# Attention scores of the next step issued ahead of the second unit's own outputs, and the output copy split in two

## The chip, the cores and the metric

The kernel runs on one core of one Trainium2 chip. The metric is the device time of one execution in microseconds, as the median of three runs.

## The reference, cut to what matters

Two blocks follow each other. The first is a chunked state-space attention over 4 batches, 8 heads, 768 positions, head size 32 and state size 16; the kernel uses chunks of 128 positions, which gives the same result as the reference's chunks of 32:

```python
L = np.exp(cum[:, :, :, None] - cum[:, :, None, :]) * causal
M = np.einsum('bhin,bhjn->bhij', Cc, Bc) * L            # scores, masked and decayed
y_intra = np.einsum('bhij,bhjd->bhid', M, xc)           # a chunk's own outputs
y_inter = np.einsum('bhin,bhnd->bhid', Cc, state) * np.exp(cum)[..., None]
y[:, :, sl] = y_intra + y_inter
state = decay_full * state + sum_j(B_j x_j decay_from_j)
```

The second is a mixture of 8 experts: each of the 3072 tokens (256 wide) goes to the one expert with the largest gate logit, and gets `relu(x @ w1[e]) @ w2[e]` times its gate probability.

## The kernel before, in words

A *unit* is one chunk of 128 positions of one batch, with all 8 heads: 24 units. A *step* `d` handles the two units `2d` and `2d+1`; there are 12 steps (`ND`), and the first `NP = 2` of them have no earlier state. The order of every instruction on every engine is the order in which the Python code issues it (`manual_schedule`); semaphores are placed by the tile framework, which follows which instruction reads or writes what part of which tile.

One step on TensorE, in the order of the code before the change:

- `rows(d-1)` (line 347 of the profile, tile `r`): the outputs of the step before, turned back to token rows and multiplied with the gate weights. It reads the tile `yT`: first the half of heads 0 to 3 (`t = 0`) for both units, then the half of heads 4 to 7 (`t = 1`).
- `y_old(d)` (line 327): the part of the outputs from the carried state, into the PSUM tile `y`; from step 2 on.
- `rank` (lines 392 to 399), in six of the steps: places of the tokens within their expert.
- `y_own(d, 0)` (line 335): the first unit's own outputs, 8 matmuls, one for each head, from `M` and the scaled inputs `xp`. Each head takes 32 of the 128 output partitions, so that four heads lie beside each other.
- `own(d)` (line 292): the new state's sum, into a free part of `y` (`A_ps`). In steps 0 and 1 it stands ahead of the own outputs, in step 11 it is left out.
- `y_own(d, 1)` (line 335): the second unit's own outputs.
- `scores(2d+2)` and `scores(2d+3)` (line 277, tile `g`): the scores of the two units of the next step, 8 matmuls on quarters of 32 rows.

The other engines around it:

- VectorE: `weigh(2d)` and `weigh(2d+1)` (line 282) take the scores from `g`, mask them and write `M`; then `rows_out(d-1)` (line 357), logits, choices and ranks.
- ScalarE: masked `C` for the next step (line 261, tile `cm`), `faded` (line 303), in steps 7 to 9 the scaled inputs of the second unit of the next step (line 269), then `turned(d)` (line 340), which copies the outputs of both units from `y` to `yT` in one instruction, and `state(d)` (line 312), four small ones that write `S`. In step 4 `turn_both(1)` transposes two tables into `y` on TensorE before that copy, and `take_both(1)` (line 225) and the copy into `ew` (line 252) follow it on ScalarE.
- GpSimd: the other scaled inputs (line 271), the state's sum (line 318), and the indirect DMAs (line 421) that put token rows into per-expert lists in HBM.
- SP: all plain loads.

`g` and `y` exist once each. `g` is laid out as four banks, each with one half for even and one half for odd units; `y` as two banks, one for each half of four heads:

```python
g_ps = ps.tile([128, 4, 2, 256], FP32, name="g")       # bank q, unit parity, 2 heads x 128
y_ps = ps.tile([128, 2, 512], FP32, name="y")          # bank t, units side by side; A_ps and tables behind
A_ps = y_ps[:, 0, 256:384]
```

After step 11 come six filler matmuls (line 135) and the experts: for each, 8 blocks of `h` (line 551) and the products with `w2` (line 586), TensorE alone setting the pace.

Of the kernel before, what the change touches and what calls it, by code (L numbers as in the profile page):

```python
# [9 lines left out]
FP32 = mybir.dt.float32  # L10
# [8 lines left out]
NB, NH, S, D, NS = 4, 8, 768, 32, 16  # L19
N, DM, E, F = 3072, 256, 8, 1024  # L20
CH = 128
NP = NB // 2
NC = S // CH
ND = NP * NC
# [7 lines left out]
KT, FT = DM // 128, F // 128  # L32
# [15 lines left out]
def ssd_then_moe(ctx, tc, xs_in, ae_in, wgx, w_gate, w1, w2, gx, gb, gc, ga, out):  # L48
    nc = tc.nc
# [14 lines left out]
    wk = att.enter_context(tc.tile_pool(name="wk", bufs=2))  # L64
# [49 lines left out]
    y_ps = ps.tile([128, 2, 512], FP32, name="y")  # L114
# [17 lines left out]
    def idle(n, to=r_ps[:, 0]):  # L132

        for _ in range(n):
            nc.tensor.matmul(to[:, 0:256], lhsT=none_bf[:, 0:128], rhs=none_bf, start=True, stop=True)
# [44 lines left out]
    sd = [dict() for _ in range(ND)]  # L180
    carry = {}

    def load(n):
        t = ld.tile([128, XW], FP32, name="xs_n")
        if n > 3:
            nc.sync.dma_start(out=t, in_=xs_in[n])
        else:
            nc.sync.dma_start(out=t[:, 384:640], in_=xs_in[n][:, 384:640])
        s_ = st[n]
        s_["t"] = t  # L190
        s_["x"] = t[:, 0:256]
        s_["B"] = t[:, 256:384]
        s_["BT"] = t[:, 384:512]
        s_["CT"] = t[:, 512:640]
# [7 lines left out]
    def load_w(e, u, q):  # L202
        n = KT * F // 4
        nc.sync.dma_start(out=w_sb[e][u][:, q * n:q * n + n], in_=(w1, w2)[u][e, :, q * n:q * n + n])
# [14 lines left out]
    def turn_both(w):  # L219
        for j, rows_ in enumerate((cum[:, w], inv)):  # L220
            nc.tensor.transpose(y_ps[:, 1, 256 + CW * j:256 + CW * j + CW], rows_, ident[0:CW, 0:CW])
# [32 lines left out]
    def masked_C(n, dve=False):  # L254
        t = wk.tile([128, 2, CH], FP32, name="cm", bufs=4)
        for u in range(2):
            if dve:
                nc.vector.tensor_scalar(out=t[:, u], in0=st[n]["CT"], scalar1=par[:, u:u + 1], scalar2=None,
                                        op0=ALU.mult)
            else:  # L260
                nc.scalar.mul(t[:, u], st[n]["CT"], par[:, u:u + 1])  # L261
        st[n]["cm"] = t

    def scaled_x(n, eng):
        t = wk.tile([128, NH, D], FP32, name="xp", bufs=4)
        st[n]["xp"] = t.rearrange("p h d -> p (h d)")
        if eng is nc.scalar:
            for h in range(NH):
                nc.scalar.mul(t[:, h], st[n]["x"][:, D * h:D * h + D], Ei[:, n, h:h + 1])
            return  # L270
        eng.tensor_tensor(out=t, in0=st[n]["x"].rearrange("p (h d) -> p h d", d=D),  # L271
                          in1=bc(Ei[:, n, :, None], [128, NH, D]), op=ALU.mult)

    def scores(n):
        for q in range(4):
            r = slice(32 * q, 32 * q + 32)
            nc.tensor.matmul(g_ps[:, q, n % 2], lhsT=st[n]["BT"][r],  # L277
                             rhs=st[n]["cm"][r].rearrange("p u i -> p (u i)"), start=True, stop=True)
# [18 lines left out]
    def faded(d):  # L297

        if d // NP == NC - 1 or d < NP:
            return  # L300
        fa = wk.tile([128, 2, 2 * D], FP32, name="fa")
        for s in range(2):
            nc.scalar.mul(fa[:, s], carry[d][:, s], ew[:, 2 * d + s:2 * d + s + 1])
        sd[d]["fa"] = fa
# [11 lines left out]
    def whole(d):  # L316
        if "fa" in sd[d]:
            nc.gpsimd.tensor_tensor(out=carry[d + NP], in0=carry[d + NP], in1=sd[d]["fa"], op=ALU.add)
# [11 lines left out]
    def y_own(d, s, heads):  # L330
        n = 2 * d + s
        first = d // NP == 0 and s == 0
        for h in heads:
            o = D * (h % 4)
            nc.tensor.matmul(y_ps[o:o + D, h // 4, CH * s:CH * s + CH], lhsT=st[n]["xp"][:, D * h:D * h + D],  # L335
                             rhs=st[n]["M"][:, h], start=first, stop=True, skip_group_check=True)

    def turned(d):
        sd[d]["yT"] = wk.tile([128, KT, 2 * CH], FP32, name="yT")
        nc.scalar.copy(out=sd[d]["yT"], in_=y_ps[:, :, 0:2 * CH])  # L340

    rt = [(sm if i < CUT else sm2).tile([128, n, W], FP32, name=f"rows{i}") for i, n in enumerate(RGS)]
    grp = [g for g, n in enumerate(RGS) for _ in range(n)]
# [1 line left out]
    def rows(d, to=None):  # L345
        for t, s in [(t, s) for t in range(KT) for s in range(2)]:
            nc.tensor.matmul((to[s] if to else r_ps[:, s])[:, 256 * t:256 * t + 160], lhsT=sd[d]["yT"][:, t, CH * s:CH * s + CH],  # L347
                                 rhs=turn[:, t].rearrange("p e h -> p (e h)"), start=True, stop=True,
                                 skip_group_check=True)
# [65 lines left out]
    def counted(g, cs):  # L415
        nc.gpsimd.tensor_tensor(out=cnt[:, g + 1, :], in0=cnt[:, g, :], in1=cs, op=ALU.add)
# [13 lines left out]
    def place(k, apart=True):  # L430
        to_places(rt[grp[k]][:, k - R0[grp[k]], :], pos[:, k:k + 1], apart)
# [282 lines left out]
    with tc.manual_schedule():  # L714
# [37 lines left out]
        for d in range(ND):  # L752
            k = d - 1
            for n in (2 * d + 6, 2 * d + 7):
                if n < NU:
                    load(n)
            for j, at in enumerate(wq):
                if at == d:
                    load_w(j // 8, j % 8 // 4, j % 4)
            def some_place(apart=False):  # L760
                if todo:
                    place(todo.pop(0), apart)

            if d == 9:
                counted(*counting.pop(0))
            some_place(d == 8)
            if d == 8:
                counted(*counting.pop(0))
            if k >= 0:
                whole(k)  # L770
            if d != 7:
                some_place()
            if d + 1 < ND:
                for s in range(2):
                    masked_C(2 * d + 2 + s)
                scaled_x(2 * d + 2, nc.gpsimd)
                if d in (6, 8):
                    some_place()
                if not 7 <= d <= 9:
                    scaled_x(2 * d + 3, nc.gpsimd)  # L780
            faded(d)
            if 7 <= d <= 9:
                scaled_x(2 * d + 3, nc.scalar)
            if k >= 0:
                rows(k)
            if d < NP:
                own(d)
            if d == 0 or d == 4:
                totals(d // 4)
            if d == 0:  # L790
                idle(3)
            y_old(d)
            q = late.get(d)
            if q is not None:
                rank(q)
                if q == CUT - 1:
                    counts(CUT)
            weigh(2 * d)
            weigh(2 * d + 1)
            if d == 0:  # L800
                take_totals(0)
                inverse(0, p0, 4, 12)
            y_own(d, 0, range(NH))
            if d >= NP:
                own(d)
            y_own(d, 1, range(NH))
            if d == 4:
                turn_both(1)
            turned(d)
            if d == 4:  # L810
                take_both(1)
            state(d)
            if d + 1 < ND:
                for s in range(2):
                    scores(2 * d + 2 + s)
            if q is not None:
                ranked(q)
                if q == CUT - 1:
                    cut()
                todo += list(range(R0[q], R0[q] + RGS[q]))  # L820
                if d == 7:
                    some_place()
            if d == ND - 1:
                m_xT(0)
            if k >= 0:
                rows_out(k)
                if d == 4:
                    take_totals(1)
            if d == 0:
                route_consts()  # L830
            if k >= 0:
                logits_of(k)
            if d in ends:
                q = ends[d]
                choose(q)
                counting.append((q, count(q)))
                if d < 7:
                    counted(*counting.pop(0))
                late[d + 1] = q
            if d == 1:  # L840
                empty_consts()
                empty_last()
                decays(1)
                lasts(1)
            if d == 3:
                inverse_rows(1)
            if d == 9:
                while todo:
                    some_place(len(todo) == 1)
            if d == 10:  # L850
                m_load(0, (nc.sync, nc.scalar))
                m_load(1)
                for k in range(8):
                    load_w(2, *divmod(k, 4))
                weakest()
# [137 lines left out]
```

## Time and profile before

| | us |
|---|---|
| median of 3 runs | 247.48 |
| lowest, highest | 246.64, 249.29 |
| the profiled execution, its own time | 247.47 |
| its span, first to last instruction | 245.8 |
| attention, steps 0 to 11, until the first expert's matmul | 0 to 60.56 of the span |

| engine | busy us | share of the span |
|---|---|---|
| TensorE, matmuls | 237.3 | 97% |
| TensorE, weight loads | 201.3 | 82% |
| ScalarE | 92.7 | 38% |
| VectorE | 88.5 | 36% |
| GpSimd | 82.8 | 34% |

Shares are averages over two very different parts: ScalarE, VectorE and GpSimd do most of their work in the first 60 us. In the timeline each line has the start, the duration (from the first to the last of the merged instructions), the engine, the line of the kernel, the operation, the tiles written and read, the size, the count, and in brackets how long the engine was idle before and what ended that. `PE` is a matmul and `PEld` the weight load that belongs to it. A float32 matmul shows as two matmuls and two weight loads, so 8 of them count as x16.

### The profile page before, as it was taken

The numbers are of one execution on the slowest core, as the hardware profiler recorded it, in microseconds if no ns is written. First come the engines' busy times: TensorE is split into PE (matmuls) and PEld (weight loads), VectorE is DVE, ScalarE is ACT, GpSimd is POOL, SyncE is SP. The second block draws the span as 40 slices with busy tenths as digits, with TensorE's granted clock in tenths as the row PEclk, the third lists the DMA queues.
The fourth block names the chain that finished last, engine by engine and source line by source line (L and its number), as shares of the span: only waits on it lengthen the run. The fifth ranks groups of instructions, "written<-read, shape, count | busy, mean of one in ns | idle before, by whom it ended". The sixth has DMA issues, their size and how long they took to land. (4 is left out here: it accounts for less than half of the span.)

```text
span 245.8 us, 5525 instructions
## 1 busy us (share of the span) xinstructions
PE 237.3 (97%) x2021; PEld 201.3 (82%) x2021; DVE 88.5 (36%) x279; ACT 92.7 (38%) x312; POOL 82.8 (34%) x144
## 2 busy tenths in 40 slices
PE   8889899999999999999999999999999999999992
PEld 5567778777888888888888888888999969989781
DVE  4699879998520222020201102052316007040000
ACT  4656768981322224141422324131432502614200
POOL 2484688880038506060413330111113012013031
PEclk9999999999999999999999999999999999999999
DMA  6999979965932278696867779454303100001001
GB/s 174 327 328 323 332 250 302 291 263 102 274 141 97 112 144 274 189 256 217 235 243 213 272 168 311 87 99 82 73 13 68 32 15 29 27 4 40 3 16 45
DMA packets 36407, 39.75 MB, mean 162 GB/s; under 512 B 21947, under 2 KB 23806, under 8 KB 36352
## 3 DMA queue, kind: packets, MB, share of 16 engines
q1 hardware_dynamic: 32816, 30.24, 43.2%
q0 software_dynamic: 2880, 8.66, 9.3%
q8 instruction: 27, 0.44, 0.7%
q10 hardware_dynamic: 656, 0.18, 0.3%
q14 instruction: 28, 0.23, 0.3%
HBM read 29.72 MB, written 9.86 MB: 161 GB/s over the span
## 5 line engine op out<-in xcount | busy, mean ns | idle before, releaser
L551 PE MATMUL h_ps<-xT,w 128*128 128x256 f32 (+3 forms) x512 | 90.0, 334 | 0.3 <-ACT hT L628 0.3
L551 PEld LDWEIGHTS h_ps<-xT,w 128*128 128x128 f32 x512 | 80.8, 190 | 7.6 <-ACT hT L628 0.7
L586 PE MATMUL y_ps<-w,hT 128*128 128x256 f32 x384 | 85.1, 380 | 0.0
L586 PEld LDWEIGHTS y_ps<-w,hT 128*128 128x128 f32 x384 | 72.6, 190 | 10.5 <-issue 0.8
L564 POOL DMA_INDIRECT out_dram<-yo,lt x24 | 23.8, 991 | 58.1 <-DVE yo L571 31.3
L509 DVE TENSOR_REDUCE t_se<-t_sub 128x1 f32<-128x8 f32 (+1 forms) x20 | 3.3, 165 | 102.8 <-ACT t_sub L507 102.8
L560 ACT ACTIVATE hT<-h_ps 128x256 f32<-128x256 f32 x64 | 24.4, 384 | 29.4 <-PE h_ps L551 28.9
L282 DVE TENSOR_TENSOR M<-g,mask 128x1024 f32<-128x1024 f32 x24 | 28.2, 1218 | 3.8 <-PE g L277 3.6
L628 ACT ACTIVATE hT<-h_ps 128x128 f32<-128x128 f32 (+2 forms) x64 | 18.0, 292 | 24.1 <-PE h_ps L551 24.1
L421 POOL DMA_INDIRECT x_hbm<-rows,pos x24 | 23.9, 994 | 9.3 <-DVE pos L408 5.3
L573 ACT ACTIVATE yo<-y_ps,t_gt 128x256 f32<-128x256 f32 x14 | 6.6, 474 | 43.2 <-PE y_ps L586 43.2
L421 POOL DMA_INDIRECT x_hbm<-zrows,rest x8 | 7.7, 962 | 35.4 <-DMA lt<-x_hbm 24.9
L335 PE MATMUL y<-M,xp 128*32 128x128 f32 x384 | 15.3, 277 | 1.6 <-DVE M L282 1.3
L347 PEld LDWEIGHTS r<-turn,yT 128*128 128x128 f32 x88 | 12.2, 189 | 4.4 <-ACT yT L340 3.0
L261 ACT ACTIVATE cm<-xs_n,par 128x128 f32<-128x128 f32 x46 | 15.1, 419 | 1.5 <-DMA xs_n<-in_xs_dram 1.5
L347 PE MATMUL r<-turn,yT 128*128 128x160 f32 x88 | 14.9, 312 | 0.7 <-ACT ew L252 0.7
L564 POOL DMA_INDIRECT out_dram<-yh,lh x4 | 3.9, 983 | 33.1 <-ACT yh L602 21.2
L277 PE MATMUL g<-cm,xs_n 32*128 32x256 f32 x192 | 15.0, 423 | 0.0
L271 POOL TENSOR_TENSOR xp<-xs_n,Ei 128x256 f32<-128x256 f32 x20 | 12.1, 617 | 6.8 <-DVE last L241 3.6
L571 DVE TENSOR_SCALAR yo<-y_ps,t_gt 128x256 f32<-128x256 f32 x10 | 4.7, 483 | 24.2 <-PE y_ps L586 24.2
L340 ACT COPY yT<-y 128x512 f32<-128x512 f32 x12 | 7.0, 586 | 16.1 <-PE y L335 14.2
L520 DVE STREAM_TRANSPOSE xT<-xb 128x512 f32<-128x512 f32 (+1 forms) x16 | 9.8, 632 | 8.6 <-DMA xb<-x_hbm 7.1
(123 smaller groups left out, 156.2 us busy)
## 6 DMA issues: line engine op xcount, KB each, us to landing
w<-in_w_dram SPq DMA_DIRECT2D x64, 256.0 KB, 5.8
xs_n<-in_xs_dram SPq DMA_DIRECT2D x20, 320.0 KB, 5.8
xb<-x_hbm SPq DMA_DIRECT2D x30, 64.0 KB, 2.3
xb<-x_hbm SPq DMA_DIRECT2D x32, 48.0 KB, 2.4
xs_n<-in_xs_dram SPq DMA_DIRECT2D x4, 192.0 KB, 3.6
x_hbm<-zrows SPq DMA_DIRECT2D x1, 672.0 KB
lt<-x_hbm SPq DMA_DIRECT2D x8, 80.0 KB, 2.7
xs_n<-in_xs_dram SPq DMA_DIRECT2D x4, 128.0 KB, 2.3
```

Of the source, the lines that this page charges most:

```text
L261: nc.scalar.mul(t[:, u], st[n]["CT"], par[:, u:u + 1])
L271: eng.tensor_tensor(out=t, in0=st[n]["x"].rearrange("p (h d) -> p h d", d=D), in1=bc(Ei[:, n, :, None], [128, NH, D]), op=ALU.mult)
L277: nc.tensor.matmul(g_ps[:, q, n % 2], lhsT=st[n]["BT"][r], rhs=st[n]["cm"][r].rearrange("p u i -> p (u i)"), start=True, stop=True)
L282: nc.vector.tensor_tensor(out=t, in0=g_ps[:, :, n % 2].rearrange("p q (u i) -> p q u i", u=2), in1=bc(mask[:, None, None, :], [128, 4, 2, ...
L335: nc.tensor.matmul(y_ps[o:o + D, h // 4, CH * s:CH * s + CH], lhsT=st[n]["xp"][:, D * h:D * h + D], rhs=st[n]["M"][:, h], start=first, sto ...
L347: nc.tensor.matmul((to[s] if to else r_ps[:, s])[:, 256 * t:256 * t + 160], lhsT=sd[d]["yT"][:, t, CH * s:CH * s + CH], rhs=turn[:, t].rea ...
L421: s_ = nc.gpsimd.indirect_dma_start(out=x_hbm[:, :], out_offset=bass.IndirectOffsetOnAxis(ap=at, axis=0), in_=row, in_offset=None)
L551: nc.tensor.matmul(p[:, 0:n], lhsT=w[:, c:c + 128], rhs=xT[:, t, 0:n], start=(t == 0), stop=(t == KT - 1))
L560: nc.scalar.activation(ex[i]["hT"][:, f, 0:n], q, func=ACT.Relu)
L564: return nc.gpsimd.indirect_dma_start(out=out[:, :], out_offset=bass.IndirectOffsetOnAxis(ap=tok, axis=0), in_=yo[:, :], in_offset=None, b ...
L586: nc.tensor.matmul(p, lhsT=ex[i]["hT"][:, f, 128 * t:128 * t + 128], rhs=w_sb[e][1][:, f * DM:f * DM + DM], start=(f == 0), stop=(f == FT ...
L628: nc.scalar.activation(ex[i + u]["hT"][:, f, 0:n], q, func=ACT.Relu)
```

## The change

On TensorE the scores of the next step now stand between `own(d)` and `y_own(d, 1)`. The second unit's own outputs are issued in two halves of four heads, and each half is followed by its own copy into `yT`: 24 copies of 256 elements in place of 12 of 512. In step 4 the two table transposes come after the second half and ahead of its copy.

```diff
-    def turned(d):
-        sd[d]["yT"] = wk.tile([128, KT, 2 * CH], FP32, name="yT")
-        nc.scalar.copy(out=sd[d]["yT"], in_=y_ps[:, :, 0:2 * CH])
+    def turned(d, t):
+
+        if t == 0:
+            sd[d]["yT"] = wk.tile([128, KT, 2 * CH], FP32, name="yT")
+        nc.scalar.copy(out=sd[d]["yT"][:, t], in_=y_ps[:, t, 0:2 * CH])
...
             y_own(d, 0, range(NH))
             if d >= NP:
                 own(d)
-            y_own(d, 1, range(NH))
-            if d == 4:
-                turn_both(1)
-            turned(d)
+            if d + 1 < ND:
+                for s in range(2):
+                    scores(2 * d + 2 + s)
+            for t in range(KT):
+                y_own(d, 1, range(4 * t, 4 * t + 4))
+                if t == 1 and d == 4:
+                    turn_both(1)
+                turned(d, t)
             if d == 4:
                 take_both(1)
             state(d)
-            if d + 1 < ND:
-                for s in range(2):
-                    scores(2 * d + 2 + s)
```

## The prediction

> **What bounds the kernel now.** I read the windows first (which stage has slack on which engine), then the waits, then the timeline of single steps. The chain that ended last holds only the final store and says nothing here.
>
> ```profile
> core 0: us, PE busy (x) PEld busy (x) DVE busy (x) ACT busy (x) POOL busy (x), PEclk, DMA share, GB/s
> ...
> 30.00:40.00 10.00, 9.85 (x190) 7.98 (x190) 8.34 (x16) 6.74 (x28) 8.45 (x13) 1.00 0.84 266
> 40.00:50.00 10.00, 10.00 (x209) 7.76 (x207) 9.45 (x22) 9.87 (x42) 8.60 (x14) 1.00 0.94 314
> ```
> ```profile
> DVE M L282 <- PE g L277: 3.6, 7, 1.0
> ...
> PEld y L335 <- DVE M L282: 2.5, 5, 0.8
> ```
>
> The attention part (to 60.56 us) is a ring of nearly equal engines: from 30 us on TensorE has almost no gap, VectorE is over 80% busy, ScalarE full between 40 and 50. The two waits are all that TensorE and VectorE lose to each other over scores and `M`: VectorE 3.6 us, TensorE 2.5 us. From 60 us on TensorE is busy without a break (its listed idle there is some 2 us in 185), so a delay of attention comes out at the end one to one. A step of the ring (step 5, then step 6 up to its second unit):
>
> ```profile
> 33.00 0.40 PEld L335 LDWEIGHTS y<-M,xp 128*32 128x32 f32 x16
> ...
> 33.60 0.74 PEld L277 LDWEIGHTS g<-cm,xs_n 32*128 32x128 f32 x16 [0.20 <-issue]
> 33.60 1.15 PE L277 MATMUL g<-cm,xs_n 32*128 32x256 f32 x16
> ...
> 33.81 0.59 ACT L340 COPY yT<-y 128x512 f32<-128x512 f32 x1 [2.08 <-PE y L335]
> ...
> 34.68 1.11 PEld L347 LDWEIGHTS r<-turn,yT 128*128 128x128 f32 x8 [0.33 <-ACT yT L340]
> ...
> 34.81 2.35 DVE L282 TENSOR_TENSOR M<-g,mask 128x1024 f32<-128x1024 f32 x2 [0.74 <-PE g L277]
> ...
> 35.96 0.42 PEld L327 LDWEIGHTS y<-xs_n,S 32*64 32x64 f32 x16 [0.17 <-issue]
> ...
> 36.56 0.38 PEld L335 LDWEIGHTS y<-M,xp 128*32 128x32 f32 x16 [0.17 <-issue]
> ...
> 36.91 0.35 PEld L292 LDWEIGHTS y<-xp,xs_n 128*32 128x32 f32 x16
> ...
> 37.22 0.38 PEld L335 LDWEIGHTS y<-M,xp 128*32 128x32 f32 x16
> ```
>
> The period 33.00 to 37.22 is TensorE's own: 0.60 own outputs, 1.08 scores, 1.28 rows, 0.60 old outputs, 0.35 first unit, 0.31 state sum, with no wait but the 0.17 to 0.33 us that an instruction with a wait costs although it is long met. The copy (33.81 to 34.40) lies wholly under the scores: the 0.33 named yT ends 0.28 us after the copy. That cover is what the change takes away.
>
> **What the Trainium skill says.** *ScalarE: Activation LUTs*, What ACT_TABLE_LOAD costs, prices an ACTIVATE with immediate scale at 186 ns + 0.833 ns per element. The trace's 512-element copy takes 586 ns (the formula: 612), so I take 586 - 256 x 0.833 = 373 ns for a half. *PSUM — Partial Sum Buffer*, PSUM bank collisions raise a hardware error, says that two engines on different banks run clean; the two halves of `y` are two banks, so the chip would let heads 4 to 7 run beside the first copy. No run here shows that, and the program doesn't use it (below). *Perfetto Trace Analysis*, Tensor Engine Instruction: a matmul's end is estimated, and its semaphore comes later. So I take start-to-start distances: second unit's first load to the copy's start is 33.00 to 33.81, and 0.71 where nothing else is late (13.46 to 14.17, steps 0 and 1).
>
> **The change, part by part.** The compiled order of the changed kernel, with each instruction's semaphores, decides two points that the diff leaves open:
>
> ```
> 112 L277 Matmult g<-cm,xs_n 128x256 [waits DMAHW3_49,DVE_49,Activation_49]
> ...
> 116 L335 Matmult y<-M,xp 32x128 x4
> 117 L335 Matmult y<-M,xp 32x128 [waits Activation_49]
> ...
> 119 L349 Matmult r<-turn,yT 128x160 [waits DVE_49]
> ...
> 121 L349 Matmult r<-turn,yT 128x160 [waits Activation_49]
> ```
>
> Counting the semaphore's values: the first score waits for `weigh(2d+1)`, the *second* unit's product, although it writes the other parity's half; and head 4 waits for the copy of heads 0 to 3, although it writes the other bank. (Both fit a tracker that sees an access as one span from first to last address.) So the scores don't fill the wait for the second `M`; they only stand ahead of 0.60 us of work. And the second half, its copy and the rows become a chain with ScalarE inside and no other TensorE work left to cover it. No DMA moves, and nothing passes SP's or GpSimd's queues.
>
> From X, the moment at which the second unit's turn comes:
> - Before: own outputs 0.60, scores 1.08, rows 1.28: old outputs of the next step at X + 2.95 (33.00 to 35.96).
> - After: 0.20 for the first score's wait and 0.74 for 16 loads; heads 0 to 3 at X + 0.94. 16 loads to the copy took 0.71; half the loads save 0.19, so the copy starts 0.52 later, X + 1.46, and ends X + 1.83. A wake-up costs 0.05 to 0.1 (rows at 30.15 after the `ew` copy's end at 30.10), so heads 4 to 7 at X + 1.89. Their issue 0.19 and a met wait 0.17: rows at X + 2.25. The first two rows' loads take 0.56; the second copy is there at 1.89 + 0.52 + 0.37 + 0.06 = X + 2.84. The other two rows start between 2.84 and 2.98 (with or without a wait's cost), take 0.56 and 0.17: old outputs at X + 3.57 to 3.71, say 3.65. **+0.70 us a step**; bounds 0.5 (wakes and waits free) and 0.9 (each 0.1 dearer).
> - Gain: the weighing can start at X + 1.4 in place of X + 1.8. It is not the bound: `M` of both units is then there by X + 3.8, and TensorE asks for them at X + 4.25 and X + 4.9.
>
> Step by step (X to the next X):
> - Step 0 (4.20): TensorE waited 0.66 for `M`, so +0.05. Step 1 (4.82): it waited 0.30, and 0.2 to 0.4 ahead of the first unit; TensorE's own 4.2 + 0.7 makes +0.1.
> - Steps 2, 3, 5, 6: no such slack, 4 x 0.70 = 2.8. (Step 3 has an unexplained 0.33 inside its scores; if it was a stall that goes, 0.33 less.)
> - Step 4: here rows wait for the copy into `ew`, behind the yT copy, the tables and `state`:
>
> ```profile
> 28.44 0.59 ACT L340 COPY yT<-y 128x512 f32<-128x512 f32 x1 [1.82 <-PE y L221]
> ...
> 29.88 0.22 ACT L252 COPY ew<-r 128x12 f32<-128x12 f32 x1
> ...
> 30.15 1.11 PEld L347 LDWEIGHTS r<-turn,yT 128*128 128x128 f32 x8 [1.07 <-ACT ew L252]
> ```
>
>   Before: X = 27.42, rows at X + 2.73. After: heads 4 to 7 at X + 1.89, transposes 0.4 later, second copy at X + 2.73, from it to the end of `ew` 1.66 - 0.21 = 1.45, rows at X + 4.23: +1.5. Nothing lies under it.
> - Steps 7 to 9 (4.5 each): ScalarE was full, with copy to copy 4.47 to 4.75. Its cycle gets the gap between the two copies: 0.89 - 0.46 + 0.52 = 0.95, then 0.25 + 0.69 + 1.18 + 0.47 + 1.70 (state, `cm`, faded, scaled inputs, next copy, from starts at 47.21 to 51.71) = 5.24. TensorE's is 4.50 + 0.70 = 5.20. Together 3 x 0.75 = 2.25.
> - Step 10 (4.26, with 0.35 of waiting for `M`): +0.35. Step 11 has no scores: before, X = 59.16 to the first expert matmul 60.56. After: heads 4 to 7 at X + 0.95, fillers at X + 1.3, their 0.55: X + 1.87, +0.45. The transpose for the experts (L520, done 1.34 after X) stays ahead.
>
> Sum 0.15 + 2.8 + 1.5 + 2.25 + 0.35 + 0.45 = **7.5 us**, all on the path. The 12 extra copies' fixed time is in it. The profiled execution took 247.47 (span 245.8 and 1.7 around it), beside a median of 247.48: **255.0 us**.
>
> **Rivals.**
> 1. *VectorE is the real bound and the earlier scores pay* (the other side). Place: the gap ahead of line 282. Price: up to the 3.6 us less the first step's 0.9, giving 244.8. For it: VectorE at 80 to 95%, and seven waits for scores. It decides only if a step's VectorE work exceeds TensorE's 4.2 to 4.5 + 0.7; it is 3.5 to 4.5 (step 5: 2.35 + 0.88 + 0.3; only step 1 reaches 4.8). 4%.
> 2. *The waits in the chain cost little*: 0.3 a step in the nine steps 2, 3, 5 to 10, and 1.0 in step 4: about 4.2 us, 251.7. For it: copy and wake-up are estimates and a matmul's end is a model. Against: two copies in sequence (0.75) are compiled in. 9%.
> 3. *ScalarE sets the pace behind the second copy*: `state` ends 1.1 after that copy's start, at X + 3.5, and old outputs wait for it; in steps 5 to 9 0.4 more each, so 257.0 to 257.5. For it: ScalarE's 9.87 of 10. 10%.
>
> **How the numbers follow.** Likeliest case 77%, 255.0. The unknowns are 0.5 to 0.9 a step over nine steps (-1.8, +1.8), step 3's gap (-0.3), step 4 (-0.4, +0.3) and ScalarE (+0.5). The range 252.0 to 257.8 holds these, most of rival 3 and some of rival 2. A measurement tells about 1% from no change: faster by more 4% (rival 1), within 3% (the low end of rival 2), slower by more 93% (the rest).
>
> **What would show it.** Right: attention ends near 68 us; per step two copies of about 0.37, 0.95 apart; rows 1.3 after the second unit's first head; line 282 hardly waiting for `g`; idle weight loads ahead of lines 335 and 349 that end on the copy; rows of step 4 at 1.5 us later from X. Wrong: if steps 5 to 10 keep a period near 4.3, the chain was covered or rival 1 holds; if `state` or `ew` releases line 327, rival 3.

## The result and the profile after

| | before | after |
|---|---|---|
| median of the runs, us | 247.08 (6 runs, 246.38 to 251.06) | 257.37 (6 runs, 256.12 to 258.61) |
| ratio | | 1.0393, 95% interval 1.0344 to 1.0442 |
| the profiled execution, us | 247.47 | 258.61, the slowest of its six |
| its span, us | 245.8 | 256.9 |
| first expert's matmul, us of the span | 60.56 | 71.45 |

The change costs 10.3 us. 255.0 us (252.0 to 257.8) had been forecast, so the measured 257.37 lies inside the range, 0.4 us below its upper end. The ratios here and below are estimated from runs in the faster of the chip's two states alone, and are not quotients of the medians. Between the two profiles the first expert starts 10.9 us later, and the span is 11.1 us longer: what is lost is lost in the attention part.

The windows of the kernel after (busy us of each engine, then clock, DMA share, GB/s):

```profile
30.00:40.00 10.00, 7.50 (x156) 5.28 (x158) 6.28 (x15) 4.53 (x19) 6.76 (x10) 1.00 0.54 178
40.00:50.00 10.00, 9.50 (x182) 6.88 (x182) 7.56 (x19) 7.51 (x31) 7.12 (x12) 1.00 0.72 239
```

In the first window, which holds step 4, no engine is full any more: TensorE 7.50 of 10, VectorE 6.28, ScalarE 4.53. In the second TensorE has 9.50, VectorE 7.56 and ScalarE 7.51. The work is the same but for 12 more copies, so what has grown is waiting. The waits of the kernel after name the links (us in total, times, longest):

```profile
PEld y L335 <- ACT yT L342: 9.2, 12, 0.8
...
PE y L335 <- ACT yT L342: 6.0, 12, 0.5
DVE M L282 <- PE g L277: 4.9, 6, 1.8
```

Twelve times, once a step, the matmuls of heads 4 to 7 stand until the copy of heads 0 to 3 is done; the kernel before has no such entry. Step 5 in the timeline of the kernel after, to be laid beside the same step of before:

```profile
37.51 0.35 PEld L292 LDWEIGHTS y<-xp,xs_n 128*32 128x32 f32 x16
...
37.95 0.74 PEld L277 LDWEIGHTS g<-cm,xs_n 32*128 32x128 f32 x16
...
39.03 0.16 PEld L335 LDWEIGHTS y<-M,xp 128*32 128x32 f32 x8 [0.33 <-issue]
39.03 0.43 PE L335 MATMUL y<-M,xp 128*32 128x128 f32 x8
39.17 2.36 DVE L282 TENSOR_TENSOR M<-g,mask 128x1024 f32<-128x1024 f32 x2 [0.30 <-PE g L277]
39.52 0.37 ACT L342 COPY yT<-y 128x256 f32<-128x256 f32 x1 [3.00 <-PE y L335]
39.95 0.16 PEld L335 LDWEIGHTS y<-M,xp 128*32 128x32 f32 x8 [0.76 <-ACT yT L342]
39.95 0.43 PE L335 MATMUL y<-M,xp 128*32 128x128 f32 x8 [0.49 <-ACT yT L342]
40.30 1.13 PEld L349 LDWEIGHTS r<-turn,yT 128*128 128x128 f32 x8 [0.20 <-issue]
40.31 1.37 PE L349 MATMUL r<-turn,yT 128*128 128x160 f32 x8
40.44 0.37 ACT L342 COPY yT<-y 128x256 f32<-128x256 f32 x1 [0.55 <-PE y L335]
...
41.65 0.45 PEld L327 LDWEIGHTS y<-xs_n,S 32*64 32x64 f32 x16 [0.22 <-issue]
```

Scores, then four heads, then 0.92 us in which TensorE has four matmuls to make and waits for ScalarE, then rows. The two copies are short (0.37 each) and ScalarE had been idle 3.00 us before the first: ScalarE isn't slow, it is asked late and with nothing beside it.

From the first unit's first head (line 335) to that of the next step, and in the last row from step 10's to the first expert's matmul:

| step | before, us | after, us | difference | forecast |
|---|---|---|---|---|
| 0, 1, 2 | 14.02 | 16.60 | +2.58, of which 1.16 is a pause in step 2 | +0.85 |
| 3 | 4.64 | 5.18 | +0.54 | +0.70 |
| 4 | 5.58 | 7.27 | +1.69 | +1.50 |
| 5, 6 | 8.72 | 10.57 | +1.85 | +1.40 |
| 7, 8, 9 | 13.15 | 15.93 | +2.78 | +2.25 |
| 10, 11 | 6.32 | 7.79 | +1.47 | +0.80 |
| sum | 52.43 | 63.34 | +10.91 | +7.50 |

The forecast counts each step from the second unit's turn to that of the next step. Counted so, the two profiles differ by the same 10.9 us in sum.

### The profile page after: what moved, and what is told of

The parts are those of the page before. It is cut to its first block, busy times and chain, and to the rows that moved or that the text cites. A ratio compares the mean times of both kernels' runs of the same rounds, so it can differ in the third digit from the quotient of the medians.

```text
span 256.9 us, 5528 instructions
## 1 busy us (share of the span) xinstructions
PE 240.8 (94%) x2021; PEld 200.9 (78%) x2021; DVE 89.1 (35%) x279; ACT 94.9 (37%) x324; POOL 82.5 (32%) x144
## 3 DMA queue, kind: packets, MB, share of 16 engines
q1 hardware_dynamic: 32816, 30.24, 40.4%
## 5 line engine op out<-in xcount | busy, mean ns | idle before, releaser
L335 PE MATMUL y<-M,xp 128*32 128x128 f32 x384 | 17.7, 281 | 6.3 <-ACT yT L342 6.0
L335 PEld LDWEIGHTS y<-M,xp 128*32 128x32 f32 x384 | 8.4, 108 | 14.4 <-ACT yT L342 9.2
L342 ACT COPY yT<-y 128x256 f32<-128x256 f32 x24 | 8.9, 372 | 24.5 <-PE y L335 21.0
```

## The experiments

The theory: the copy lost its cover under the scores, and the wait of heads 4 to 7 for the first copy puts one more round trip between TensorE and ScalarE into each step. The rivals: only one of these two costs anything; or the loss is on VectorE or ScalarE. The first four kernels ran on one chip (median of the kernel before in the same rounds: 248.12 us), the next four on another (247.99). "Between state sums" below means from the first weight load of line 292 in one step to that in the next.

### The scores ahead, in one piece

```diff
             if d >= NP:
                 own(d)
+            if d + 1 < ND:
+                for s in range(2):
+                    scores(2 * d + 2 + s)
             y_own(d, 1, range(NH))
...
             state(d)
-            if d + 1 < ND:
-                for s in range(2):
-                    scores(2 * d + 2 + s)
```

> One half of the change alone: the scores stand ahead of the second unit's own outputs, which are made in one go and copied by one copy of 512 elements. Theory (the copy loses its cover under the scores, and TensorE has nothing else to do until the rows can start): from the second unit's turn X, heads at X+1.21, copy from X+1.92 to X+2.51, rows at X+2.57, next old outputs at X+3.86, which is nearly the changed kernel's X+3.83. So 256 to 258 us, within 1 us of the changed kernel, step period 5.1 to 5.2 us in step 5; step 4 about 0.4 us shorter than in the changed kernel. Rival (the halves with their wait between them are what costs, the order of the scores is neutral): 247 to 249 us.

Measured: 256.55 us, ratio 1.0319 (1.0253 to 1.0384). Its step 6:

```profile
42.40 0.35 PEld L292 LDWEIGHTS y<-xp,xs_n 128*32 128x32 f32 x16
...
42.84 0.74 PEld L277 LDWEIGHTS g<-cm,xs_n 32*128 32x128 f32 x16
...
43.92 0.38 PEld L335 LDWEIGHTS y<-M,xp 128*32 128x32 f32 x16 [0.33 <-issue]
...
44.63 0.58 ACT L340 COPY yT<-y 128x512 f32<-128x512 f32 x1 [2.17 <-PE y L335]
45.27 1.11 PEld L347 LDWEIGHTS r<-turn,yT 128*128 128x128 f32 x8 [0.97 <-ACT yT L340]
```

The rows wait 0.97 us for the one copy. From line 292 to the old outputs (46.55) it is 4.15 us; the kernel after takes 4.14 for the same stretch of its step 6 (42.63 to 46.77). So moving the scores is enough for the loss of a step, and the halves, as built, win nothing of it back. The rival is out.

Two expected numbers were missed in this profile, and both fall where TensorE's granted clock was low: 0.59, 0.50, 0.50 and 0.70 in the four microseconds from 34 to 38, and 1.00 on both sides. Step 5, between state sums, took 5.38 us, not 5.1 to 5.2. Its state sums lie in the slow stretch and took 0.62 us in place of 0.35, which is the whole difference:

```profile
37.02 0.62 PEld L292 LDWEIGHTS y<-xp,xs_n 128*32 128x32 f32 x16
```

Step 4 was to be 0.4 us shorter than in the kernel after and is 7.92 us against 7.27. Up to its rows, ahead of the slow stretch, it is shorter: 4.21 us (29.10 to 33.31) against 4.70 (30.24 to 34.94).

### The halves, scores where they were

Against the kernel after:

```diff
             if d >= NP:
                 own(d)
-            if d + 1 < ND:
-                for s in range(2):
-                    scores(2 * d + 2 + s)
             for t in range(KT):
                 y_own(d, 1, range(4 * t, 4 * t + 4))
...
             state(d)
+            if d + 1 < ND:
+                for s in range(2):
+                    scores(2 * d + 2 + s)
```

> The other half alone: own outputs and copies in halves, scores behind them as before the change. Theory (heads 4 to 7 wait for the first copy, with no work of TensorE's in between): copy from X+0.49 to X+0.86, heads 4 to 7 at X+0.92, scores at X+1.27 in place of X+0.6, the second copy hidden under the scores, rows at X+2.35 in place of X+1.67: +0.7 us a step where TensorE has no slack, 252.5 to 254.5 us in all. Rival (only the moved scores matter): 247 to 248.5 us.

Measured: 254.43 us, ratio 1.0250 (1.0200 to 1.0300). The wait of heads 4 to 7 is there in each step (9.8 us of weight loads, 12 times), and step 5 grows from 4.19 to 4.91 us between its state sums and the next (34.27 to 39.18): the 0.7 expected. So this wait costs by itself, without the moved scores. Alone the two parts cost 3.2% and 2.5%, together 3.9%, less than their sum. That one round trip between TensorE and ScalarE serves for both in the whole change would fit this; it was not tried by itself.

### The whole change with two tiles for the two halves

Against the kernel after; the other places that name `y_ps` change in the same way:

```diff
-    y_ps = ps.tile([128, 2, 512], FP32, name="y")
+    y_h = [ps.tile([128, 512], FP32, name=f"y{t}") for t in range(2)]
...
-            nc.tensor.matmul(y_ps[o:o + D, h // 4, CH * s:CH * s + CH], lhsT=st[n]["xp"][:, D * h:D * h + D],
+            nc.tensor.matmul(y_h[h // 4][o:o + D, CH * s:CH * s + CH], lhsT=st[n]["xp"][:, D * h:D * h + D],
...
-        nc.scalar.copy(out=sd[d]["yT"][:, t], in_=y_ps[:, t, 0:2 * CH])
+        nc.scalar.copy(out=sd[d]["yT"][:, t], in_=y_h[t][:, 0:2 * CH])
```

> The whole change, but the PSUM tile y is made as two tiles of one bank each, one for each half of four heads, so that heads 4 to 7 need not wait for the copy of heads 0 to 3. Theory (that wait is part of the chain, the bank rule does not need it): heads 4 to 7 right behind heads 0 to 3, rows at about X+2.15 in place of X+2.48, next old outputs at X+3.5 in place of X+3.83: 0.35 us a step less, 253 to 254.5 us. Still slower than before the change by some 6 us, since the copies have no cover. Rival (the second copy decides, whatever heads 4 to 7 wait for): 256.5 to 258 us. Rival (all of the loss is this wait): about 248 us.

Measured: 253.81 us, ratio 1.0207 (1.0142 to 1.0273). Its step 5:

```profile
35.03 0.38 PEld L335 LDWEIGHTS y<-M,xp 128*32 128x32 f32 x16 [0.33 <-issue]
35.03 0.64 PE L335 MATMUL y<-M,xp 128*32 128x128 f32 x16
...
35.53 0.65 ACT L342 COPY yT<-y 128x256 f32<-128x256 f32 x2 [3.00 <-PE y L335]
35.95 1.11 PEld L349 LDWEIGHTS r<-turn,yT 128*128 128x128 f32 x8 [0.54 <-ACT yT L342]
```

All eight heads run on, and heads 4 to 7 wait for no copy. With X at 33.82 (the state sums start at 33.51 and take 0.31) rows stand at X + 2.13, old outputs at X + 3.41; 2.15 and 3.5 were expected. The 0.54 us for which the rows still wait is what the lost cover costs here. The wait of heads 4 to 7 was therefore needed by the tracking of one tile, not by the data.

But the gain at the end was less than the steps gave. One reason is that the first expert now waited 2.14 us:

```profile
60.16 1.89 ACTq L487 DMA_DIRECT2D xb<-x_hbm  x2
...
64.92 0.71 DVE L522 STREAM_TRANSPOSE xT<-xb 128x512 f32<-128x512 f32 x1 [3.29 <-DMA xb<-x_hbm]
65.69 1.78 PEld L553 LDWEIGHTS h_ps<-xT,w 128*128 128x128 f32 x8 [2.14 <-DVE xT L522]
```

In this profile, the slowest of the kernel's four runs, the granted clock then fell to 0.52, 0.50, 0.50 and 0.78 in the microseconds from 67 to 71. From the first expert's start to the end of the span are 187.4 us, in the kernel before 185.2. Why the clock fell is open: in another profile of the changed kernel it fell after a wait of the same length, but not after two longer ones.

The kernel after shows the same, less openly:

```profile
66.78 0.37 ACT L342 COPY yT<-y 128x256 f32<-128x256 f32 x1 [0.55 <-PE y L335]
67.09 1.11 ACTq L487 DMA_DIRECT2D xb<-x_hbm  x2
...
71.45 0.73 PEld L553 LDWEIGHTS h_ps<-xT,w 128*128 128x128 f32 x4 [0.60 <-DVE xT L522]
```

Two of the four loads of the first expert's tokens are issued by ScalarE, behind step 10's last copy (66.78) and in its order. SP had issued the other two at 63.97, 3.1 us earlier; in the kernel before the two engines issued them at 55.85 and 56.00.

### The changed kernel with step 4's table copy on VectorE

```diff
-        nc.scalar.copy(ew[:, 12 * w:12 * w + 12], p)
+        (nc.vector.tensor_copy if w else nc.scalar.copy)(ew[:, 12 * w:12 * w + 12], p)
```

> The whole change, but in step 4 the copy into ew is made by VectorE right behind the instruction ahead of it, in place of ScalarE behind both yT copies, the tables and the state. Theory (step 4's rows wait for that chain): step 4's period from 7.3 to about 5.9 us, 255.7 to 256.5 us, 1.3 us less than the changed kernel, all of it in step 4. Rival (step 4 is late for another reason, the tables' transposes or the second copy): within 0.3 us of the changed kernel. A pause of 1.2 us of TensorE inside step 2's state sums, which the changed kernel's profile shows with no wait, should come again in the profiles of these four kernels if it belongs to the order of the instructions, and be elsewhere or gone if it is chance.

Measured: 255.94 us, ratio 1.0321 (1.0255 to 1.0387), against 1.0393 of the change; the two intervals overlap, so it is the step that shows the gain. Step 4, between its state sums and the next: 6.02 us (28.17 to 34.19), in the kernel after 7.27 (30.24 to 37.51). In the kernel after the rows wait 1.71 us of weight loads for `ew`; here they have no wait:

```profile
34.94 1.11 PEld L349 LDWEIGHTS r<-turn,yT 128*128 128x128 f32 x8 [1.71 <-ACT ew L252]
```
```profile
28.23 0.16 DVE L252 COPY ew<-r 128x12 f32<-128x12 f32 x1
...
31.10 1.27 PEld L349 LDWEIGHTS r<-turn,yT 128*128 128x128 f32 x8
```

(the first line is from the kernel after, the others are from this one). The pause in step 2 is missing here, although TensorE's order is the same.

### The halves in two tiles, scores where they were

This is the kernel of the second experiment with the two tiles of the third.

> Own outputs and copies in halves, in two tiles of one bank each, with the scores behind them as before the change. Theory (the loss is made of two things, the cover lost and the wait of heads 4 to 7; with neither of them, halves cost only ScalarE's second fixed time of about 0.15 us in steps 7 to 9): 247 to 249 us, within 1% of the kernel before. Rival (the split itself costs TensorE, or the copies on ScalarE hold the ring up): 250 us or more.

Measured: 247.45 us, ratio 0.9989 (0.9964 to 1.0014). Its step 5:

```profile
32.06 0.65 ACT L342 COPY yT<-y 128x256 f32<-128x256 f32 x2 [1.79 <-PE y L335]
32.14 0.74 PEld L277 LDWEIGHTS g<-cm,xs_n 32*128 32x128 f32 x16 [0.20 <-issue]
...
33.22 1.11 PEld L349 LDWEIGHTS r<-turn,yT 128*128 128x128 f32 x8 [0.33 <-issue]
```

Both copies, 0.65 us together against 0.59 for one, lie under the scores. With the cover kept and the wait taken away the loss is gone: the two named causes, with what follows from them in step 4 and at the first expert, are the whole of it, and 12 more copies cost nothing measurable.

### The first expert's loads on SP

```diff
-                m_load(0, (nc.sync, nc.scalar))
+                m_load(0)
```

On top of the whole change in two tiles.

> The whole change in two tiles of one bank, and all four loads of the first expert's tokens issued by SP (two of them were issued by ScalarE, in its order behind step 10's second copy). Theory (the later second copy held those two loads back: they were issued 2 to 3 us after SP's, and the first expert's transpose waited for them): the 2.1 us for which TensorE waited for that transpose in the version with two tiles go nearly wholly, 251.5 to 252.5 us, first expert matmul at 63.5 to 64.0. Rival (the rows were not in HBM earlier, or SP's own issue is the limit): 253.3 to 254.3 us, and the wait stays over 1.5 us.

Measured: 251.21 us, ratio 1.0137 (1.0081 to 1.0194).

```profile
58.68 2.76 SPq L487 DMA_DIRECT2D xb<-x_hbm  x4
...
63.15 0.71 DVE L522 STREAM_TRANSPOSE xT<-xb 128x512 f32<-128x512 f32 x1 [0.83 <-DMA xb<-x_hbm]
...
64.26 0.73 PEld L553 LDWEIGHTS h_ps<-xT,w 128*128 128x128 f32 x4
```

The transpose is done (63.86) before TensorE comes, and the wait for it is gone: ScalarE's place in the order held the loads back. The total came out a little below the expected 251.5 to 252.5, and the first expert a little later than 63.5 to 64.0: it starts 1.4 us earlier than in the version with two tiles, not 2.1, because attention itself ended 0.7 us later in this profile (the fillers start at 63.69, there at 63.00). The rest of the difference between the two profiles lies behind the first expert, where this one has no stretch of low clock.

### Both mended, the scores still ahead

The kernel of the experiment just above, with step 4's table copy on VectorE.

> The version with two tiles and all four loads on SP, and besides step 4's copy into ew made by VectorE. Theory (the terms add up: what is left is the lost cover, about 0.5 us a step in ten steps less the slack of the first two): 1.2 to 1.5 us less than the version with two tiles and SP's loads, 250.2 to 251.2 us, still 3 us slower than the kernel before. Rival (moving the scores ahead is harmless once all late waits are gone): 247 to 248.5 us.

Measured: 250.40 us, ratio 1.0077 (1.0042 to 1.0113). The step from 251.21 is 0.8 us, less than the 1.2 to 1.5 expected; step 4 itself is 1.16 us shorter (6.58 to 5.42 between state sums), and this profile has longer pauses of TensorE with no wait (1.03 us in step 2, 0.83 ahead of step 10) than the other one (0.22 in step 2). The rows still wait for the first copy in ten steps, 5.5 us in all, and a step like step 5 takes 4.68 us between state sums where the kernel before has 4.19. So what remains is the moved scores, 0.8% slower than before: moving them is not harmless once the rest is mended. The kernel before with all loads on SP was not run, so what that edit does by itself is not known.

### Versions that beat both

The kernel before, with step 4's table copy on VectorE:

> The kernel before the change, with only step 4's copy into ew made by VectorE right behind the instruction ahead of it. Theory: the 1.07 us that TensorE's weight loads waited there shrink to the 0.2 to 0.3 of a wait that is met, so 0.7 to 0.9 us less, 246.2 to 247.2 us where the kernel before has 247 to 248: a version that beats both. Rival (step 5 gives it back, as the state's sum or the second unit is late): within 0.2 us of the kernel before.

Measured: 246.83 us, ratio 0.9969 (0.9944 to 0.9995). Step 4 takes 4.85 us between state sums (25.60 to 30.45), before 5.58; the rows' idle falls from 1.07 to 0.33 us. Both kernels are beaten, the one before by only 0.3%, with an interval that ends just short of no change.

With the halves in two tiles besides:

> Halves in two tiles with the scores behind them, and step 4's copy into ew made by VectorE: the two edits that cost nothing or gained. Theory (step 4's wait of 0.85 us goes, the halves stay free): 246.2 to 247.2 us, at or just below the version of before with the copy on VectorE. Rival (both gains are one and the same, since an earlier second copy already shortened step 4's chain): 247.2 to 248 us, as the halves alone.

> The changed kernel once more, for a second profile. If the pause of TensorE of 1.2 us in step 2 is chance, it is missing or elsewhere, and step 2 takes 5.3 to 5.5 us from first unit to first unit in place of 6.7; 256 to 257.5 us. If it belongs to the kernel, it stands in step 2 again.

These two ran on another chip, on which the kernel before has 254.26 us, so only the ratios say something. The halves with the table copy: 252.90, ratio 0.9927 (0.9893 to 0.9962), clear of no change; whether it is better than the table copy alone is open, as the two never ran on the same chip. The changed kernel: 268.72, ratio 1.0539 (1.0491 to 1.0586), more than the 1.0393 above; the expected 256 to 257.5 us were meant for the earlier chips. In its profile heads 4 to 7 wait up to 2.4 us of weight loads for the first copy: twice (3.8 us in sum) ScalarE stood idle ahead of that copy, released by no engine of this core that the profile names. At the first of the two VectorE, waiting for TensorE, went on at the same moment (52.54), so it is not settled which engine was late. TensorE, with nothing to cover the chain, waited along. The granted clock was also lower there: 0.977 to 0.989 in the runs of the changed kernel that the ratio uses, 0.988 to 1.000 in those of the kernel before, and 0.50 for some 3 us behind a first expert that waited 2.14 us. So the larger ratio is not a cost of the change alone.

In step 2 TensorE pauses again, 0.61 us, at the same place as in the first profile: inside the state sums, after five of their sixteen weight loads. Of the seven profiles with the scores ahead four have a pause there (1.16, 0.61, 1.03 and 0.22 us), of the five with the scores behind none. That speaks against mere chance, but the length is not fixed, and the cause was not found.

## Why the prediction was right, point by point

The mechanism was right: the copies lost their cover, and heads 4 to 7 wait for the first copy. The sum was too low. Of the 3.4 us that the profile has above it, 1.16 are the pause in step 2, 0.6 the rest of the first three steps, 1.0 steps 5 to 9 and 0.7 the last two; steps 3 and 4 cancel. It is partly luck that the number stays inside the range, and the number alone would even speak for the third rival (257.0 to 257.5), whose wait the profile does not show.

- **The two waits read from the compiled order** (the first score waits for the second unit's product, head 4 for the first copy): right. Line 335 waits for the copy twelve times, and the version with two tiles takes that wait away for 0.44 us in step 5 (5.12 to 4.68 between state sums).
- **The chain from the second unit's turn**: its later part was right to 0.1 us. From heads 0 to 3 to heads 4 to 7 0.92 us (forecast 0.95), a half copy 0.37 (0.373), to the rows 0.35 (0.36), to the old outputs 1.35 (1.40).
- **The term that was too small** is the one ahead of it, "0.20 for the first score's wait and 0.74 for 16 loads". The scores hold TensorE for 1.08 us until the next weight load, not 0.74. I had taken the 0.33 us after them in the profile of before as the price of the rows' met wait, which would go with that wait. It stayed, named "issue", ahead of line 335, which waits for nothing there. That is +0.34, against 0.07 too much for the first wait and 0.1 too much later: a step costs +0.9, not +0.70. In steps 5 to 9 this is 1.0 us.
- **Steps 0 to 2** came to +1.4 without the pause, for +0.85. Step 0 alone, from first unit to first unit, took 0.8 us longer (8.11 to 13.16, before 8.13 to 12.39), where the waits for `M` had been expected to hide almost all of it.
- **Step 3's unexplained 0.33** was listed as a stall that may go. It went: +0.54 in place of +0.9.
- **Step 4** measured +1.69 for +1.5, and the experiment on the table copy gives 1.25 of it back in that step, so the place was right.
- **Steps 7 to 9**: +0.93 each like steps 5 and 6, so ScalarE's fuller cycle in these steps did not add to TensorE's.
- **Steps 10 and 11**: +1.47 for +0.80. "No DMA moves" was wrong: the two loads in ScalarE's order are issued behind the later copy, and for the transpose that I said "stays ahead" TensorE waited 0.60 us, before 0.24. In the version with two tiles the same wait is 2.14. The other 0.3 us is step 10, +0.7 for +0.35: its waiting for `M` did not pay for half of the loss, as I had assumed.
- **The pause of 1.16 us** in step 2 was not in the sum. This profile is of the slowest of the six runs; the median is 1.2 us lower. Whether the faster runs have the pause is not on record.
- **Rivals**: VectorE's gain did not come. It waits 4.9 us for scores, before 3.6, as TensorE's ring is longer; "hardly waiting" was wrong. The cheap chain (251.7) is out. ScalarE's `state` does end 1.10 us after the second copy's start, as the third rival says (40.44 to 41.54 in step 5), but line 327 then stands only 0.22 us idle in place of the 0.17 of before, so it costs some 0.05 us a step, not 0.4.

## What to carry to other kernels

When work is moved ahead, ask what it lay beside before: here the scores were the cover of a copy, and none of the versions with the scores ahead made good for it (the best is 0.8% slower). Read the compiled waits of a change that splits a tile: halves of one tile may still be chained, and one tile for each half made them run side by side. Where an engine with other work also issues DMAs, look at what stands ahead of them in its order: here the loads of ScalarE were issued 3.1 us after those of SP.

## What the runs showed of the hardware

- After the scores, matmuls on quarters of 32 rows with 256 columns, the next weight load over all 128 rows starts 0.33 us after the last of theirs, whether it has a wait (rows, in the kernel before) or none (line 335, in all six kernels with the scores ahead). After line 327, also on quarters of 32 rows but with 128 columns, the same gap is 0.17 us. The Trainium skill, *TensorE: Matmul & The Clock Gate*, Part 3, The mechanism, says that a weight load overlaps matmuls in flight only where the row group differs. That would fit the gap, but as it stands the sentence does not fit this trace: in the experts matmuls and weight loads both cover all 128 rows, and from 80 to 100 us of the kernel before the profile has the matmuls busy for 20.00 us and the weight loads for 17.53 beside them. So the reason of the gap is open.
- Two copies of 256 elements behind each other take 0.65 us where one of 512 takes 0.59: cutting a copy on ScalarE costs 0.06 us if nothing stands between.
- A ScalarE read of PSUM runs beside TensorE's writes to other banks with both at their usual times: in the kernel before the copy out of `y` (33.81 to 34.40) lies inside the scores into `g` (weight loads 33.60 to 34.34). The Trainium skill, *PSUM — Partial Sum Buffer*, PSUM bank collisions raise a hardware error, says so of different banks. For the two banks of `y` the version with two tiles shows it only by the profile's estimate of a matmul's end: the first copy starts at 35.53, the last matmul is put to end at 35.67.
